# Moving the cast, the transposes and the load of the coming batches of x to a later place in one step of a fused attention and gated-FFN kernel

## Chip, cores and metric

The kernel runs on one core of one Trainium2 chip. The metric is the device time of one launch in microseconds (us), as the median of several runs. A profiled execution gives a trace beside it: what each engine did, and the core's span from the first to the last instruction.

## What is computed

For each of 8 batches x has 8 heads of 512 rows of 64 values, and a state has 8 heads of 32 rows. The attention goes both ways, and its joined result (544 rows a batch, 512 wide) goes through a gated FFN with 1536 hidden columns. Cut from the reference:

```python
scores = scale * np.matmul(x, state.transpose(0, 1, 3, 2))
a = softmax(scores)                      # x reads the state
xread = np.matmul(a, state)
scores2 = scale * np.matmul(state, x.transpose(0, 1, 3, 2))
a2 = softmax(scores2)                    # the state reads x
sread = np.matmul(a2, x)
x = concatenate([xread, sread], axis=2)  # then (batch, row, head * dim)
gate = 1.0 / (1.0 + np.exp(-(x @ w_gate)))
val = x @ w_val
out = (gate * val) @ w_out
```

`softmax` stands here for the maximum, exponential, sum and division of the original.

## The kernel before, in words

The rows that read the state are never multiplied with w_gate and w_val as rows of `xread`. The kernel forms `SW` (state times gate and value weights, `sw_wide`) for a batch, and multiplies it with the transposed attention `aT` (`gv_mm`, L283). So `gv_mm` of a batch needs that batch's `SW` and `aT`. Tanh on ScalarE (`gv_th`, L293) and a multiply on VectorE (`gv_glu`, L298) give `glu`, and `out_mm` (L314) multiplies it with w_out. The rows of all states' reads (`XS`) are a ninth batch at the end.

The order of the work is written out by hand. A first list (L425 to L690) handles batches 0 and 1 and the start of batch 2. Then a loop (L692) runs one step for each batch b from 2 to 8. A step has 12 groups, f = 0 to 11, one for each 128 hidden columns. A group issues `gv_mm(b, f)`, its tanh and multiply, and a third of a row block of `out_mm` of batch b - 1; where f is 0 or 6, half of `SW` of the next batch, nb = b + 1, comes first. Between them the step prepares the coming batches:

- `row(nb, t)`, six parts, t = 0 to 5: the scores (`S_mm`, L121, one half in t = 0 and the other in t = 1), maximum, subtraction and exponential, the sums and reciprocals (`n_sum`, L144 and L146), the multiply on GpSimd that gives `ab` (`n_mul`, L152), and last `aT_dma` (L173): four DMA transposes on SyncE's queue (SP), from `ab` to `aT`.
- `col(nb, t)`, five parts in f = 7 to 11: the scores the other way (`cT_mm`), exponential, a normalising multiply on GpSimd (`cT_nrm`, L204), and `c_dma` (L209): two DMA transposes on SP.
- `cast_x(nb + 1)`, two casts on GpSimd (L91) that wait for the load of that batch's x, and `at_xT_dma(nb + 1)`, four DMA transposes on SP (L113) that wait for the casts. Their result `xT` is what `S_mm` of that batch reads in the next step.
- `load_x(nb + 2)`, the load of a batch of x (1 MB, L74) on SP.
- `sr_mm(b)` and `sr_cp(b)`: the read of the state, 16 matmuls and two small copies.

In this trace GpSimd and SP's queue run their instructions in the order in which the list issues them, so one that waits holds up all that stand behind it. Outputs (`out_mm`, every third group) are also stored through SP (L320). In step 2 the code before has the groups of `row(3)` at f = 1 to 6, the casts and the transposes of batch 4 at f = 1, the load of batch 5 at f = 6. In step 3 it has `row(4)` at f = 0 to 5, the casts and the transposes of batch 5 at f = 1, and `sr_mm(3)` at f = 3 in the PSUM pool that the first scores use (`AT`). The load of batch 4 is issued just ahead of step 2 (L689).

Of the kernel before, what the change touches and what calls it, by code (L numbers as in the profile page):

```python
# [16 lines left out]
def kernel(  # L17
# [15 lines left out]
    B, H, S, D = x.shape  # L33
# [30 lines left out]
    AT, OU, GV, SWP = (p_at, "at"), (p_out, "outp"), (p_gv, "gv"), (p_sw, "swp")  # L64
# [5 lines left out]
    def load_x(b, eng, parts=1):  # L70
        xf = xfs[b] = stg.tile((128, H, 4, D), FP, name="xf")
        v, n = x[b].rearrange("h (p c) d -> p h c d", c=4), H // parts
        for i in range(parts):
            eng.dma_start(xf[:, n * i:n * i + n], v[:, n * i:n * i + n])  # L74
# [40 lines left out]
    def S_mm(b, i, place, jjs=(0, 1)):  # L115
        if jjs[0] == 0:
            held["S", b, i] = place[0].tile((128, 4, 2, 2, Ns), FP, name="Sp", tag=place[1])
        ps = held["S", b, i]
        for jj in jjs:
            for c in range(4):  # L120
                nc.tensor.matmul(ps[:, c, :, jj], xTs[b][:, 2 * i + jj, c], sTz[:, b, 2 * i + jj], start=True, stop=True)  # L121

    def S_max(b, i):

        if b not in E1s:
            E1s[b] = ap_.tile((128, 4, 2, 4, Ns), FP, name="E1")
        ps = held["S", b, i].rearrange("p c e j n -> p (c e) j n")
        mx = held["mx", b, i] = ap_.tile((128, 8, 2), FP, name="mx")
        nc.vector.tensor_reduce(mx, ps, AX.X, ALU.max)  # L129

    def S_sub(b, i):

        mx, ps = held["mx", b, i], held["S", b, i].rearrange("p c e j n -> p (c e) j n")
        nc.vector.tensor_tensor(halfE(b, i), ps, mx.unsqueeze(3).to_broadcast((128, 8, 2, Ns)), ALU.subtract)  # L134

    def S_exp(b, i):
        nc.scalar.activation(halfE(b, i), halfE(b, i), AF.Exp, scale=scale)  # L137
# [4 lines left out]
    def n_sum(b, i):  # L142
        rs = ap_.tile((128, 8, 2), FP, name="rs")
        nc.vector.tensor_reduce(rs, halfE(b, i), AX.X, ALU.add)  # L144
        ri = held["ri", b, i] = ap_.tile((128, 8, 2), FP, name="ri")
        nc.vector.reciprocal(ri, rs)  # L146

    def n_mul(b, i, eng, lo=0, n=4):
        if b not in abs_:
            abs_[b] = ap_.tile((128, 4, 2, 128), BF, name="ab")  # L150
        ri, ce = held["ri", b, i], slice(2 * lo, 2 * lo + 2 * n)
        eng.tensor_tensor(abs_[b].rearrange("p c e (j n) -> p (c e) j n", n=Ns)[:, ce, 2 * i:2 * i + 2],  # L152
                          halfE(b, i)[:, ce], ri[:, ce].unsqueeze(3).to_broadcast((128, 2 * n, 2, Ns)), ALU.mult)
# [17 lines left out]
    def aT_dma(b):  # L171
        for c in range(4):
            nc.sync.dma_start_transpose(aT_tile(b)[:, c], abs_[b][:, c].rearrange("p e k -> p (e k)"))  # L173
# [37 lines left out]
    def sr_mm(b, place):  # L211
        sr = held["sr", b] = place[0].tile((128, 4, 2, Ns), FP, name="srp", tag=place[1])
        Eb = Ebs[b].rearrange("p c e (j n) -> p c e j n", n=Ns)
        for j in range(4):
            for c in range(4):
                nc.tensor.matmul(sr[:, j], xbs[b][:, c, 2 * j:2 * j + 2].rearrange("p h d -> p (h d)"),  # L216
                                 Eb[:, c, :, j], start=(c == 0), stop=(c == 3))

    def sr_cp(b, e, cp):
        rows = slice(e * 64, (e + 1) * 64)  # L220
        cp(XS[rows, :, b * Ns:(b + 1) * Ns], held["sr", b][rows, :, e])
# [28 lines left out]
    def sw_wide(b, v):  # L250

        if b not in SWs:
            SWs[b] = fp.tile((128, 2, 2, dff), BF, name="SW", bufs=2)
        lo = 768 * v
        for k, places in enumerate(((OU, AT), (SWP, SWP), (SWP, SWP))):
            pss = [p[0].tile((128, 512), FP, name="swp", tag=p[1]) for p in places]
            if k < 2:
                sw_mm(pss, b, k, lo, 512, 0)
            else:
                for w in range(2):  # L260
                    sw_mm(pss, b, w, lo + 512, 256, 256 * w)
            for e in range(2):
                if k < 2:
                    sw_left[b, v, k, e] = (SWs[b][:, e, k, lo:lo + 512], pss[e])
                else:
                    sw_left[b, v, k, e] = (SWs[b][:, e, :, lo + 512:lo + 768], pss[e].rearrange("p (w n) -> p w n", w=2))

    def sw_cp(b, lo, w, e, cp):
        cp(*sw_left.pop((b, lo, w, e)))  # L269
# [5 lines left out]
    def gv_mm(b, f, place):  # L275
        n = n_of(b)
        fs = slice(f * 128, (f + 1) * 128)
        pss = []
        for w in range(2):
            ps = place[0].tile((128, 512), FP, name="gvp", tag=place[1])[:, :n]  # L280
            if b < B:
                for g in range(2):
                    nc.tensor.matmul(ps, SWs[b][:, g, w, fs], aTs[b][:, :, g], start=(g == 0), stop=(g == 1))  # L283
            else:
                for j in range(4):
                    nc.tensor.matmul(ps, (wg, wv)[w][:, j, fs], XS[:, j], start=(j == 0), stop=(j == 3))  # L286
            pss.append(ps)
        held["gv", b, f] = pss

    def gv_th(b, f):  # L290

        th = held["th", b, f] = fp.tile((128, 512), FP, name="th")[:, :n_of(b)]
        nc.scalar.activation(th, held["gv", b, f][0], AF.Tanh, scale=0.5)  # L293

    def gv_glu(b, f):
        if b not in glus:
            glus[b] = fp.tile((128, NF, n_of(b)), BF, name="glu", bufs=2, padded_shape=(128, NF, 512))
        nc.vector.scalar_tensor_tensor(glus[b][:, f], held["th", b, f], 1.0, held["gv", b, f][1], ALU.add, ALU.mult)  # L298
# [102 lines left out]
    def row(b, t):  # L401

        if t == 0:
            S_mm(b, 0, AT)
            S_max(b, 0)
        elif t == 1:
            S_sub(b, 0)
            S_mm(b, 1, SWP)
            S_max(b, 1)
        elif t == 2:  # L410
            S_sub(b, 1)
            S_exp(b, 0)
        elif t == 3:
            S_exp(b, 1)
            n_sum(b, 0)
            n_mul(b, 0, nc.gpsimd)
        elif t == 4:
            n_sum(b, 1)
            n_mul(b, 1, nc.gpsimd)
        else:  # L420
            aT_dma(b)
# [270 lines left out]
    for b in range(2, B + 1):  # L692
        nb = b + 1 if b + 1 < B else None
        for f in range(NF):

            v, q = divmod(f, 6)
            if nb is not None and q == 0:
                sw_wide(nb, v)
                sw_cp(nb, v, 0, 0, act)
                sw_cp(nb, v, 0, 1, act)  # L700
            ahead = nb is not None and q == 0
            for first in (ahead, not ahead):
                if first:
                    gv_mm(b, f, SWP if b == B and f % 2 else GV)
                    gv_th(b, f)
                    gv_glu(b, f)
                elif b < B or f < 9:
                    out_mm(b - 1, f)
            if nb is not None:
                if q == 0:  # L710
                    sw_cp(nb, v, 1, 0, vec)
                if q in (1, 3, 4):
                    k = max(q + 1, 3)
                    sw_cp(nb, v, k // 2, k % 2, act)
                if f == (4 if b > 2 else 10):
                    sr_cp(b, 0, act)
                    sr_cp(b, 1, vec)
                if 0 <= f - (b == 2) < 6:
                    row(nb, f - (b == 2))
                elif f >= 7:  # L720
                    col(nb, f - 7)
                if f == 6 and nb + 2 < B:
                    load_x(nb + 2, nc.sync, 4 if nb + 3 == B else 1)
                if f == 1 and nb + 1 < B:
                    cast_x(nb + 1, pool, 0, 4)
                    cast_x(nb + 1, pool, 4, 4)
                    at_xT_dma(nb + 1)
            if b < B and f == (3 if b > 2 else 9):
                sr_mm(b, AT if b > 2 else SWP)
            if b == B - 1:  # L730
                if f == 4:
                    sr_cp(b, 0, act)
                    sr_cp(b, 1, vec)
                for k in range(2):
                    if 0 <= f - 3 * k < 5:
                        col(k, f - 3 * k)
                    elif f == 8 + 3 * k:
                        sr_mm(k, SWP)
                        sr_cp(k, 0, act)
                        sr_cp(k, 1, vec)  # L740
# [33 lines left out]
```

## Time and profile before

| | us |
|---|---|
| median of 3 runs | 236.31 |
| lowest, highest | 235.29, 237.57 |
| the profiled execution, device time | 237.39 |
| its span, first to last instruction | 235.6 |
| TensorE busy in it | 224.3 |
| VectorE, ScalarE, GpSimd busy | 139.6, 144.0, 68.5 |

The device time of the profiled execution is 1.8 us more than its span, and 1.1 us more than the median of the runs. In the rows that follow, PE is TensorE, DVE is VectorE, ACT is ScalarE, POOL is GpSimd, and SPq is SyncE's DMA queue. A row of a timeline gives the start in us, the duration in us, the engine, the line of the kernel, the operation, output and input, the number of instructions, and in brackets the idle time before it with what ended it. The granted clock (PEclk) is the share of TensorE's full clock that it was given.

### The profile page before, as it was taken

Reading aid. Unit: us, or ns where it says so; the run is one execution under the profiler, and the core shown is the slowest. Engines: PE = TensorE matmul, PEld = TensorE weight load, DVE = VectorE, ACT = ScalarE, POOL = GpSimd, SP = SyncE. Lnnn points to the kernel's source line nnn. Section 1 sums busy time; section 2 is a strip of 40 time slices with the busy share of each in tenths; the row PEclk is TensorE's granted clock in tenths of the full one; section 3 lists DMA queues with packets and bytes.
Section 4 is the critical chain, followed back from the end, with each engine's and each line's share of the span. In section 5 each row is a group of like instructions: output and inputs, shape, how many; then the busy total and the mean of one; then the engine's idle time right before and its main releaser. Section 6 shows DMA issues by size and latency. Waiting matters only on the chain.

```text
span 235.6 us, 4975 instructions
## 1 busy us (share of the span) xinstructions
PE 224.3 (95%) x1887; PEld 112.4 (48%) x1887; DVE 139.6 (59%) x267; ACT 144.0 (61%) x290; POOL 68.5 (29%) x74
## 2 busy tenths in 40 slices
PE   5798999999999959999999999999999999999994
PEld 4674434444444424444444444444444444566754
DVE  3599889946586526754774567556765664432211
ACT  3679777957585825848485857585748555432311
POOL 4876180062024143303520261113110426100001
PEclk9999999999999979999999999999999999999999
DMA  6999969817553458527451665214122312311104
GB/s 205 273 200 289 180 99 188 236 36 200 127 177 67 136 138 220 156 49 268 83 143 37 178 167 123 69 56 92 46 70 67 90 57 79 89 45 67 69 22 114
DMA packets 47271, 29.49 MB, mean 125 GB/s; under 512 B 29872, under 2 KB 42544, under 8 KB 47248
## 3 DMA queue, kind: packets, MB, share of 16 engines
q1 hardware_dynamic: 40096, 21.84, 34.0%
q0 software_dynamic: 6864, 7.14, 16.4%
q10 hardware_dynamic: 288, 0.20, 0.5%
q8 instruction: 15, 0.25, 0.5%
q14 instruction: 8, 0.07, 0.1%
HBM read 18.35 MB, written 8.91 MB: 116 GB/s over the span
## 4 chain that ended last, share of the span: by engine, by line
PE 79%; DVE 6%; ACT 4%; DMA 3%; SPq 3%; issue 2%; POOL 2%; ACTq 0%; DVEq 0%; POOLq 0%
PE outp L314 33%; PE gvp L283 30%; PE gvp L286 5%; PE swp L231 4%; DVE glu L298 3%; DMA xf<-in_x_dram 2%; SPq L173 2%; ACT th L293 2%; PE Sp L121 2%; PE srp L216 1%; PE warm L348 1%; DVE rs L144 1%; PE outp L334 1%; PE cTp L181 1%; DMA aT<-ab 1%
## 5 line engine op out<-in xcount | busy, mean ns | idle before, releaser
L298 DVE SCALAR_TENSOR_TENSOR glu<-th,gvp 128x512 bf16<-128x512 f32 (+1 forms) x108 | 70.2, 657 | 72.2 <-ACT th L293 52.1
L283 PE MATMUL gvp<-aT,SW 128*128 128x512 bf16 x384 | 97.5, 379 | 3.3 <-DMA aT<-ab 2.5
L314 PE MATMUL outp<-wo,glu 128*128 128x512 bf16 x396 | 100.4, 384 | 0.0
L293 ACT ACTIVATE th<-gvp 128x512 f32<-128x512 f32 (+1 forms) x108 | 61.4, 575 | 56.2 <-PE gvp L283 46.7
L283 PEld LDWEIGHTS <-SW 128*128 128x128 bf16 x384 | 36.3, 98 | 49.3 <-issue 8.9
L314 PEld LDWEIGHTS <-glu 128*128 128x128 bf16 x396 | 37.1, 98 | 41.3 <-issue 3.4
L269 ACT CAST SW<-swp 128x512 bf16<-128x512 f32 x74 | 41.1, 587 | 4.0 <-PE swp L231 2.9
L204 POOL TENSOR_SCALAR cN<-cE,rc 128x512 bf16<-128x512 f32 x16 | 25.0, 1565 | 59.1 <-DVE rc L201 57.4
L318 ACT ACTIVATE res<-outp 128x512 f32<-128x512 f32 x33 | 19.7, 597 | 17.2 <-PE outp L314 17.0
L152 POOL TENSOR_TENSOR ab<-E,ri 128x512 bf16<-128x512 f32 x14 | 14.6, 1048 | 32.1 <-ACT E L137 15.3
L91 POOL CAST xb<-xf 128x1024 bf16<-128x1024 f32 (+1 forms) x13 | 12.5, 977 | 33.1 <-DMA xf<-in_x_dram 27.8
L269 DVE CAST SW<-swp 128x512 bf16<-128x512 f32 x22 | 14.7, 681 | 3.6 <-PE swp L231 3.6
L196 ACT ACTIVATE cE<-cTp,nb 128x512 f32<-128x512 f32 x16 | 11.1, 693 | 1.2 <-POOL cN L204 1.2
L129 DVE TENSOR_REDUCE mx<-Sp 128x16 f32<-128x512 f32 x16 | 10.9, 679 | 1.1 <-PE Sp L121 1.1
L134 DVE TENSOR_TENSOR E<-Sp,mx 128x512 f32<-128x512 f32 x16 | 11.0, 686 | 0.2
L188 DVE TENSOR_REDUCE cm<-cTp 128x1 f32<-128x512 f32 x16 | 10.9, 683 | 0.0
L144 DVE TENSOR_REDUCE rs<-E 128x16 f32<-128x512 f32 x16 | 10.8, 678 | 0.1
L137 ACT ACTIVATE E<-E 128x512 f32<-128x512 f32 x16 | 10.2, 639 | 0.5 <-DVE E L134 0.5
L325 POOL DMA_DIRECT2D out_dram<-res x2 | 1.1, 554 | 29.7 <-ACT res L318 29.7
L231 PE MATMUL swp<-wg,sTc 64*32 64x512 bf16 (+1 forms) x192 | 8.4, 328 | 0.1
L121 PEld LDWEIGHTS <-xT 128*128 128x128 bf16 x128 | 6.8, 108 | 3.2 <-issue 0.8
L231 PEld LDWEIGHTS <-sTc 64*32 64x32 bf16 x384 | 4.6, 91 | 7.4 <-issue 5.1
(62 smaller groups left out, 140.3 us busy)
## 6 DMA issues: line engine op xcount, KB each, us to landing
out_dram<-res SPq DMA_DIRECT2D x31, 256.0 KB, 2.4
xf<-in_x_dram SPq DMA_DIRECT2D x12, 256.0 KB, 4.6
xf<-in_x_dram SPq DMA_DIRECT2D x3, 1024.0 KB, 6.1
wo<-in_moe_w_out_dram POOLq DMA_DIRECT2D x3, 512.0 KB, 8.0
wv<-in_moe_w_val_dram POOLq DMA_DIRECT2D x2, 512.0 KB, 10.1
wg<-in_moe_w_gate_dram POOLq DMA_DIRECT2D x2, 512.0 KB, 9.8
xf<-in_x_dram POOLq DMA_DIRECT2D x2, 512.0 KB, 7.8
xf<-in_x_dram POOLq DMA_DIRECT2D x1, 1024.0 KB, 13.4
```

The costliest lines, as they stand in the source:

```text
L91: cp(xbs[b].rearrange("p c h d -> p h c d")[:, lo:lo + n], xfs[b][:, lo:lo + n])
L144: nc.vector.tensor_reduce(rs, halfE(b, i), AX.X, ALU.add)
L152: eng.tensor_tensor(abs_[b].rearrange("p c e (j n) -> p (c e) j n", n=Ns)[:, ce, 2 * i:2 * i + 2], halfE(b, i)[:, ce], ri[:, ce].unsqueeze ...
L204: eng.tensor_scalar(held["cN", b][:, e], held["cE", b, e], rc, None, op0=ALU.mult)
L231: nc.tensor.matmul(pss[e][j * Ns:(j + 1) * Ns, o:o + n], sTc[rows, b, j] if b > 1 else sTz[rows, b, j, e], (wg, wv)[w][rows, j, lo:lo + n] ...
L269: cp(*sw_left.pop((b, lo, w, e)))
L283: nc.tensor.matmul(ps, SWs[b][:, g, w, fs], aTs[b][:, :, g], start=(g == 0), stop=(g == 1))
L286: nc.tensor.matmul(ps, (wg, wv)[w][:, j, fs], XS[:, j], start=(j == 0), stop=(j == 3))
L293: nc.scalar.activation(th, held["gv", b, f][0], AF.Tanh, scale=0.5)
L298: nc.vector.scalar_tensor_tensor(glus[b][:, f], held["th", b, f], 1.0, held["gv", b, f][1], ALU.add, ALU.mult)
L314: nc.tensor.matmul(ops[b, c], glus[b][:, f, c * 128:(c + 1) * 128], wo[:, f], start=(f == 0), stop=(f == NF - 1))
L318: nc.scalar.activation(res, ops[b, c], AF.Copy, scale=0.5)
```

## The change

Only the loop changes. In step 2 the casts and transposes of x of batch 4 move from f = 1 to f = 6, where they stand behind `aT_dma(3)`, and the load of batch 5 moves from f = 6 to f = 8. In step 3 `row(4)` moves from f = 0 to 5 to f = 1 to 6, `sr_mm(3)` from f = 3 to f = 9 and from the pool `AT` to `SWP`, and `sr_cp(3)` from f = 4 to f = 10. All other steps stay. No instruction is added or taken away.

```diff
-                if f == (4 if b > 2 else 10):
+                if f == (4 if b > 3 else 10):
                     sr_cp(b, 0, act)
                     sr_cp(b, 1, vec)
-                if 0 <= f - (b == 2) < 6:
-                    row(nb, f - (b == 2))
+                if 0 <= f - (b < 4) < 6:
+                    row(nb, f - (b < 4))
                 elif f >= 7:
                     col(nb, f - 7)
-                if f == 6 and nb + 2 < B:
+                if f == (6 if b > 2 else 8) and nb + 2 < B:
                     load_x(nb + 2, nc.sync, 4 if nb + 3 == B else 1)
-                if f == 1 and nb + 1 < B:
+                if f == (1 if b > 2 else 6) and nb + 1 < B:
                     cast_x(nb + 1, pool, 0, 4)
                     cast_x(nb + 1, pool, 4, 4)
                     at_xT_dma(nb + 1)
-            if b < B and f == (3 if b > 2 else 9):
-                sr_mm(b, AT if b > 2 else SWP)
+            if b < B and f == (3 if b > 3 else 9):
+                sr_mm(b, AT if b > 3 else SWP)
```

In the issue order of the engines this gives, for steps 2 and 3: on POOL the two multiplies (L152) of batch 3 now stand ahead of the two casts of batch 4. On SP the order before was load 4, four transposes xT(4), two stores, four transposes aT(3), load 5, two stores, two transposes of batch 3's other scores, four transposes xT(5). It becomes load 4, two stores, four transposes aT(3), four transposes xT(4), a store, load 5, a store, two transposes of batch 3's other scores, four transposes xT(5).

## Prediction

> **What bounds the kernel now.** I read the page first, then TensorE's waits, then the chain of waits around the one long wait, then the clock in that place.
>
> ```profile
> span 235.6 us, 4975 instructions
> PE 224.3 (95%) x1887; PEld 112.4 (48%) x1887; DVE 139.6 (59%) x267; ACT 144.0 (61%) x290; POOL 68.5 (29%) x74
> PEclk9999999999999979999999999999999999999999
> PE 79%; DVE 6%; ACT 4%; DMA 3%; SPq 3%; issue 2%; POOL 2%; ACTq 0%; DVEq 0%; POOLq 0%
> ```
>
> TensorE is the bound: 95% busy, 79% of the chain that ended last. One slice of the clock's 40 stands at 7, the fifteenth, from 82.5 to 88.4 us. TensorE's own waits name the cause:
>
> ```profile
> PE gvp L283 <- DMA aT<-ab: 2.5, 1, 2.5
> ```
>
> That is the longest wait of TensorE in the run, and it happens once, at the start of step 3. The chain shows it:
>
> ```profile
> 82.58 2.38 DMA aT<-ab
> ...
> 85.09 1.02 PE gvp L283 x4
> 86.11 1.70 PE outp L314 x4
> ...
> 88.24 1.50 PE outp L314 x4
> 89.74 0.86 PE gvp L283 x4
> ```
>
> The last transpose of aT(3) is issued at 82.58 and lands 2.38 us later; `gv_mm(3, 0)` starts at 85.09. Then four output matmuls take 1.70 and 1.50 us, where four take 0.86 elsewhere. So the wait is paid twice: idle, and then at a low clock. The windows give the clock:
>
> ```profile
> 85.00:88.00 3.00, 2.91 (x16) 1.37 (x17) 1.29 (x2) 0.60 (x1) 0.00 (x0) 0.67 0.69 205
> 88.00:91.00 3.00, 3.00 (x23) 1.45 (x21) 0.85 (x2) 0.79 (x2) 0.82 (x1) 0.77 1.03 333
> ```
>
> After the stretch the columns are its length, the five engines' busy time, the clock (0.67, 0.77), the DMA share and GB/s. The loss is 3.0 x 0.33 + 3.0 x 0.23 = 1.68 us.
>
> Why aT(3) is late stands in SP's queue:
>
> ```profile
> 63.20 0.57 SPq L74 DMA_DIRECT2D xf<-in_x_dram  x1
> 71.45 5.13 SPq L113 DMA_TRANSPOSE xT<-xb  x4
> 76.68 1.00 SPq L320 DMA_DIRECT2D out_dram<-res  x2
> 77.78 6.04 SPq L173 DMA_TRANSPOSE aT<-ab  x4
> 83.93 0.52 SPq L74 DMA_DIRECT2D xf<-in_x_dram  x1
> ...
> 92.23 5.12 SPq L113 DMA_TRANSPOSE xT<-xb  x4
> 97.45 1.00 SPq L320 DMA_DIRECT2D out_dram<-res  x2
> 100.09 5.05 SPq L173 DMA_TRANSPOSE aT<-ab  x4
> ```
>
> Load 4 (63.20) is awaited by the casts; SP stands at the transposes of xT(4) until 71.45, spends 5.13 us issuing them and 1.00 on two stores, and only at 77.78 starts aT(3). GpSimd has the same knot:
>
> ```profile
> 69.40 2.02 POOL L91 CAST xb<-xf 128x1024 bf16<-128x1024 f32 x2 [14.38 <-DMA xf<-in_x_dram]
> 71.39 2.06 POOL L152 TENSOR_TENSOR ab<-E,ri 128x512 bf16<-128x512 f32 x2
> 90.18 2.02 POOL L91 CAST xb<-xf 128x1024 bf16<-128x1024 f32 x2 [5.33 <-PE gvp L283]
> 99.01 1.05 POOL L152 TENSOR_TENSOR ab<-E,ri 128x512 bf16<-128x512 f32 x1 [1.59 <-DVE ri L146]
> ```
>
> **The change part by part.** First, aT(3) goes ahead of xT(4). VectorE gives the last reciprocal that `ab` needs here:
>
> ```profile
> 71.36 0.25 DVE L146 RECIPROCAL ri<-rs 128x16 f32<-128x16 f32 x1
> ```
>
> It ends at 71.61, and 0.15 us later (as 98.61 + 0.25 to 99.01 has it in the next step) the second multiply can start; the first, free of the casts, is done by then. At 1.05 us each `ab` is ready at 72.8, against 73.45 before. The two stores of the step's early groups are gone by then: the second's result is written here,
>
> ```profile
> 68.92 0.60 ACT L318 ACTIVATE res<-outp 128x512 f32<-128x512 f32 x1
> ```
>
> and a store's issue takes 0.5. SP starts aT(3) at 72.9. Its fourth issue begins 3.9 us later, at 76.8, and lands 2.4 later, at 79.2. The four swp groups end at 85.09 - 2.52 = 82.57, so the slack is 3.4 us where 2.52 was missing. The whole wait goes, and with it the low clock that followed.
>
> Second, xT(4) goes behind it. The casts on GpSimd start at 72.8 (load 4 had landed by 69.40) and end at 74.8, hidden behind SP's issue of aT(3), which ends at 78.0. The transposes run from 78.1 to 83.2; the fourth is issued at about 82.0 and lands at 84.5. Who needs it is `S_mm(4, 0)`, now in group 1 of step 3. What TensorE does in the steps:
>
> ```profile
> 58.49 1.04 PE L283 MATMUL gvp<-aT,SW 128*128 128x512 bf16 x4
> ...
> 61.95 0.40 PE L121 MATMUL Sp<-sTz,xT 128*128 128x64 bf16 x8
> ...
> 81.72 0.41 PE L231 MATMUL swp<-wg,sTc 64*32 64x512 bf16 x8
> ...
> 85.09 1.02 PE L283 MATMUL gvp<-aT,SW 128*128 128x512 bf16 x4 [2.52 <-DMA aT<-ab]
> ```
> ```profile
> 110.10 0.41 PE L231 MATMUL swp<-wg,sTc 64*32 64x512 bf16 x8
> ...
> 110.88 1.04 PE L283 MATMUL gvp<-aT,SW 128*128 128x512 bf16 x4
> ...
> 134.24 0.41 PE L231 MATMUL swp<-wg,sTc 64*32 64x512 bf16 x8
> ```
>
> In step 2 the scores in group 1 come 61.95 - 58.49 = 3.46 us after the step's first matmul. In step 3 they are then due at 82.57 + 3.46 = 86.0: slack 1.5 us. Cost nothing, but this is what is late next.
>
> Third, load 5 moves behind xT(4) and a store: 83.2 + 0.6 = 83.8, where it started at 83.93. So its landing, the casts at 90.18, xT(5) at 92.23 and the two stores to 98.45 stay. `ab` of batch 4 was ready at 100.06 (99.01 + 1.05); with the row of step 2's pattern it comes 72.8 - 58.49 = 14.3 us after the step's start, at 96.9. So SP sets aT(4): issued from 98.5, its fourth at 102.3, landed at 104.7. It is due at 82.57 + 23.23 + 0.78 = 106.6 (the step's length is next; 0.78 is 110.88 - 110.10). Slack 1.9 us, where it was 4.6. Cost nothing.
>
> Fourth, the row and `sr` of step 3 take step 2's places. From first gv to the next step's swp: step 2 took 81.72 - 58.49 = 23.23, step 3 took 110.10 - 85.09 = 25.01, step 4 took 134.24 - 110.88 = 23.36. Step 3 is 1.65 longer than step 4, the low clock by another road (1.68 above). The new pattern is worth 23.36 - 23.23 = 0.13 more. It could cost instead: step 2's neighbours differ, so I bound it by -0.13 and +0.13 and take the gain, since the issue order of step 3 becomes that of step 2.
>
> The sum: 2.52 idle + 1.65 clock + 0.13 = 4.30 us. The span becomes 231.3, the profiled execution 237.39 - 4.30 = 233.1. That execution lay 1.08 above the median of the runs, so for the median 236.31 - 4.30 = 232.0 us.
>
> The Trainium skill, page "TensorE: Matmul & The Clock Gate", section "Why this matters for your kernels", speaks against the second term: to keep the clock, no idle gaps over about 3 us between bursts, since one idle window halves it. This trace differs: a gap of 2.52 us was followed by clocks of 0.67 and 0.77. By that rule the clock would not be at stake and the gain would be 2.65.
>
> **The rivals.**
> A, the forecast: 232.0.
>
> B, the low clock is not there in most runs. It shows in one execution, which lay above the median, and the three runs spread over 2.3 us. Then only 2.52 + 0.13 goes: 236.31 - 2.65 = 233.7. Against it: the trace has the low clock right behind the gap, and the clock is full in the steps beside it. The same page ("What's actually happening") says that the window runs free of the kernel, so whether a gap is caught varies; no run here shows that yet.
>
> C, SP is late and another wait takes the place of the one removed. Four transposes do not always take 5.05:
>
> ```profile
> 172.50 6.21 SPq L173 DMA_TRANSPOSE aT<-ab  x4
> ```
> ```profile
> DMA to landing us min/median/max: 2.4/2.5/4.2
> ```
>
> The first row is of SP's queue for aT(7), the second of the xT transposes, from issue to landing. Were aT(3) and xT(4) both 1.16 longer, xT(4) would land at 86.8, 0.8 late; with the longest landing, 1.7 more, 2.5 late. `gv_mm(4, 0)` with its 1.9 slack has four such groups ahead: if three are long, 3.5 - 1.9 = 1.6 late. So 0.8 to 2.5 us comes back: 232.8 to 234.5, about 233.5 in the middle. Against it: both have over 1 us in hand at the usual durations.
>
> D, slower. Load 5 lands late and, as GpSimd and SP both wait for it in order, `ab` and aT(4) come late with it.
>
> ```profile
> xf<-in_x_dram SPq DMA_DIRECT2D x3, 1024.0 KB, 6.1
> ...
> xf<-in_x_dram POOLq DMA_DIRECT2D x1, 1024.0 KB, 13.4
> ```
>
> If it took 13.4 us, 7.3 more, TensorE would wait 7.3 - 1.9 = 5.4 at step 4 and lose the clock's 1.65 again: 7.0 - 4.3 = 2.7 slower, 239.0. It decides from 4.3 - 1.65 + 1.9 = 4.6 us of delay. Against it: SP's own loads take 6.1, the slow one was another queue's, and load 5 is issued at the same moment as before with the same neighbours.
>
> E, no change: aT(3) is late for another reason than its place in the queue. Against it: SP's order, GpSimd's order and the reciprocal's end leave none. 236.3.
>
> **How the numbers follow.** A 0.66, B 0.14, C 0.12, D 0.05, E 0.03. The forecast is A: 232.0. The range reaches down 1.0 for the spread of medians (the runs shown differ by 2.3) and up to 234.4, which takes in B and nearly all of C; D, E and the edges, under 2 in 10, are left out. A measurement of this kernel can tell about 1% from no change, 2.4 us. Faster by more (below 233.9): A, two thirds of B and half of C, 0.82. Within 1%: the rest of B and C and E, 0.13. Slower: D, 0.05.
>
> **What would show it.** Step 1 is right if the wait of `gvp` for aT is gone and the first gv of step 3 starts right behind the swp, near 82.6; the clock of the following windows is then 1.00. Step 2 is right if the scores in group 1 of step 3 start without a wait of TensorE for xT. Step 3 is right if load 5 is issued near 83.8 and the first gv of step 4 waits for nothing, near 106.6. Step 4 is right if step 3 takes 23.2 from gv to swp. A wait of TensorE in group 1 of step 3 or at the start of step 4 would be C or D; a slow clock elsewhere, or a median near 233.7 with the gap gone, would be B.

## The result and the profile after

The changed kernel takes 234.65 us (median of 11 runs, 233.37 to 235.43), the kernel before 236.69 in the same comparison: a ratio of 0.9911, with a 95% interval of 0.9883 to 0.9939. That is 2.1 us faster, where 4.3 were forecast; 234.65 lies above the range. Some executions of both kernels run in a slower state (in one trace of the kernel before the clock is 0.95 nearly from end to end); the ratios, their intervals and the counts of runs below leave them out, the medians in us do not.

The profiled execution after took 233.37 us, which makes it the fastest of the 11 runs. Three lines of its page:

```profile
span 231.5 us, 4975 instructions
PE 221.2 (96%) x1887; PEld 110.0 (48%) x1887; DVE 139.2 (60%) x267; ACT 144.0 (62%) x290; POOL 68.6 (30%) x74
PEclk9999999999999999999999999999999999999999
```

The 7 in the clock's row is gone. SP's queue after (start, duration, line, operation):

```profile
72.31 5.04 SPq L173 DMA_TRANSPOSE aT<-ab  x4
77.45 5.75 SPq L113 DMA_TRANSPOSE xT<-xb  x4
...
83.94 0.39 SPq L74 DMA_DIRECT2D xf<-in_x_dram  x1
...
92.52 5.45 SPq L113 DMA_TRANSPOSE xT<-xb  x4
...
99.17 5.07 SPq L173 DMA_TRANSPOSE aT<-ab  x4
104.35 0.52 SPq L74 DMA_DIRECT2D xf<-in_x_dram  x1
...
106.81 3.23 SPq L209 DMA_TRANSPOSE Eb<-cN  x2
```

The order is the one of the change: aT(3) at 72.31, then xT(4), then load 5 at 83.94. TensorE's timeline after, at the places that the prediction named:

```profile
57.19 0.41 PE L231 MATMUL swp<-wg,sTc 64*32 64x512 bf16 x8
57.97 1.04 PE L283 MATMUL gvp<-aT,SW 128*128 128x512 bf16 x4
...
81.98 1.04 PE L283 MATMUL gvp<-aT,SW 128*128 128x512 bf16 x4
...
85.44 0.40 PE L121 MATMUL Sp<-sTz,xT 128*128 128x64 bf16 x8
...
105.21 0.41 PE L231 MATMUL swp<-wg,sTc 64*32 64x512 bf16 x8
...
105.99 1.04 PE L283 MATMUL gvp<-aT,SW 128*128 128x512 bf16 x4
...
114.18 0.63 PE L216 MATMUL srp<-Eb,xb 128*128 128x64 bf16 x16 [0.65 <-DMA Eb<-cN]
```

From the first gv of step 2 to that of step 4 it takes 105.99 - 57.97 = 48.02 us; before it took 110.88 - 58.49 = 52.39. So the four steps of the prediction brought 4.37 us in this execution, against 4.30 worked out. The last row is new: in group 3 of step 4 the read of the state by batch 4 (`sr_mm(4)`) waits for the two transposes of its `Eb`. The read is also shown before the change, with SP's queue and the time from issue to landing of its two transposes:

```profile
105.25 0.52 SPq L74 DMA_DIRECT2D xf<-in_x_dram  x1
...
111.25 3.30 SPq L209 DMA_TRANSPOSE Eb<-cN  x2
```
```profile
DMA to landing us min/median/max: 2.7/3.4/4.0
```
```profile
118.26 0.63 PE L216 MATMUL srp<-Eb,xb 128*128 128x64 bf16 x16
```

Before, the second of the two is issued at 112.99 and lands 2.7 us later, at 115.7, so the read has 2.6 us in hand. The rest of the question is what the new wait costs, and what other executions look like.

### The profile page after: what moved, and what is told of

Read it like the earlier page. It is cut to its first block, busy times and chain, and to the rows that moved or that the text cites. A ratio compares the mean times of both kernels' runs of the same rounds, so it can differ in the third digit from the quotient of the medians.

```text
span 231.5 us, 4975 instructions
## 1 busy us (share of the span) xinstructions
PE 221.2 (96%) x1887; PEld 110.0 (48%) x1887; DVE 139.2 (60%) x267; ACT 144.0 (62%) x290; POOL 68.6 (30%) x74
## 4 chain that ended last, share of the span: by engine, by line
PE 74%; DMA 9%; ACT 6%; DVE 3%; POOL 3%; issue 2%; SPq 1%; ACTq 0%; POOLq 0%; DVEq 0%
PE outp L314 33%; PE gvp L283 27%; PE gvp L286 5%; DMA wo<-in_moe_w_out_dram 4%; PE swp L231 4%; DMA xf<-in_x_dram 2%; DMA Eb<-cN 2%; DVE glu L298 2%; PE srp L216 2%; ACT th L293 1%; POOL cN L204 1%; ACT SW L269 1%; ACT E L137 1%; PE cTp L181 1%; PE outp L334 1%
## 5 line engine op out<-in xcount | busy, mean ns | idle before, releaser
L314 PE MATMUL outp<-wo,glu 128*128 128x512 bf16 x396 | 98.9, 379 | 0.4 <-DMA wo<-in_moe_w_out_dram 0.4
L152 POOL TENSOR_TENSOR ab<-E,ri 128x512 bf16<-128x512 f32 x14 | 14.6, 1048 | 40.3 <-DVE ri L146 29.8
L121 PEld LDWEIGHTS <-xT 128*128 128x128 bf16 x128 | 6.3, 103 | 3.2 <-ACT xT L108 0.4
```

Source lines behind the costliest of these rows:

```text
L314: nc.tensor.matmul(ops[b, c], glus[b][:, f, c * 128:(c + 1) * 128], wo[:, f], start=(f == 0), stop=(f == NF - 1))
```

## The experiments

Each ratio compares a kernel with the kernel before on the same chip; the chips differ from one group of experiments to the next.

**The kernel before once more, and a filled gap.** The first was unchanged.

> The kernel before, unchanged, for a second trace and the granted clock of each run. Two theories for why the median fell by about 2.1 us (0.9911 of 236.69) where steps 2 to 4 of the two traces differ by 4.37 - 0.80 = 3.57 us. Theory W (a new wait): every execution of the kernel before has the wait of about 2.5 us and the low clock; then the mean clock of nearly all runs is near 0.993, as in the first trace (1.68 us of 235.6 is 0.7%), and the second trace has a wait of 2.2 us or more. Theory V (the removed cost varies): in most executions TensorE reaches step 3 later against SP's queue, the wait is shorter and often leaves the clock alone; then most runs have a mean clock of 0.997 or more, and the second trace has a wait under 2 us or no window below 0.95 behind it.

Measured: 0.9985 (0.9949 to 1.0022). Of the 22 runs of the kernel before on the other side of this comparison, 15 had a mean clock of 0.991 to 0.993 and 7 one of 0.999 or 1.000. Of the 9 on this side, the same kernel, 3 had a low one; on two other chips it was 13 of 17 and 10 of 16. So about two executions in three (41 of 64) pay the low clock, neither all nor few. A second trace:

> The kernel before once more, one look. Its wait for aT of batch 3 at the start of step 3: 2.0 to 3.5 us, and a granted clock under 0.9 in one of the two windows of 3 us behind it, as about three quarters of its runs have a mean clock near 0.992. A trace with a mean clock of 1.000 would show what the wait is where the clock is kept.

Measured: 236.38 us, mean clock 0.992, and this wait, and these windows (length, five engines' busy time, clock, DMA share, GB/s):

```profile
PE gvp L283 <- DMA aT<-ab: 2.4, 1, 2.4
```
```profile
84.00:87.00 3.00, 2.71 (x7) 1.02 (x8) 0.74 (x2) 0.60 (x1) 0.17 (x1) 0.50 0.70 204
87.00:90.00 3.00, 3.00 (x29) 1.55 (x27) 1.35 (x3) 0.74 (x2) 0.60 (x1) 0.93 0.94 308
```

The clock loses 3.0 x 0.50 + 3.0 x 0.07 = 1.7 us, as in the first trace. The filled gap:

```diff
+            if b == 3 and f == 0:
+                warm(20, GV)
             ahead = nb is not None and q == 0
```

> The kernel before with 20 matmuls of 128 columns on constants (about 0.1 us each, 2.0 us) put into the place where TensorE waits for aT of batch 3; their result is read by nothing. The wait for aT stays, TensorE is busy in it, so the clock should not fall. It measures the clock term alone. If the low clock comes in every execution (theory W): 1.65 us faster, 0.993. If it comes in few (theory V): within 0.5 us of the kernel before, 0.998 to 1.003, or slower where the wait is shorter than 2.0 us.

Measured: 235.11 us, 0.9940 (0.9912 to 0.9968), 1.4 us faster. The 20 matmuls take 1.3 us instead of the 2.0 estimated. The trace keeps a clock of 1.00 in the window behind the gap although TensorE still waits there:

```profile
PE gvp L283 <- DMA aT<-ab: 1.3, 1, 1.3
```
```profile
85.00:88.00 3.00, 3.00 (x29) 1.64 (x28) 2.06 (x5) 1.07 (x2) 0.00 (x0) 1.00 0.93 317
```

So work that computes nothing, put into an idle stretch, makes this kernel faster. The clock term was real: 1.4 us of the median, where one execution showed 1.65. Part of what the clock was worth is already given back here: in this trace the read of batch 3 waits 0.57 us for its `Eb`, a wait that neither of the two traces of the kernel before shown here has.

**The changed kernel in more executions.**

> The changed kernel, unchanged, for a second trace. Its first trace is of its fastest run (233.37, median 234.65) and has a wait of 0.65 us of TensorE in step 4, where the 16 matmuls of the state's read of batch 4 wait for transposes that were issued behind load 6. Theory W: in a run near the median that wait is longer, 1.5 to 2.5 us. Theory V: it stays at 0.3 to 1.2 us, and the runs differ ahead of step 2, in the first list: the start of step 2, 57.97 in the first trace, moves by 1 us or more. Against the kernel before: 0.985 to 0.995 by both.

Measured: 0.9924 (0.9889 to 0.9959); the traced execution took 234.96 us. Its timeline of TensorE and SP's queue:

```profile
56.89 0.41 PE L231 MATMUL swp<-wg,sTc 64*32 64x512 bf16 x8
...
107.92 1.02 PE L283 MATMUL gvp<-aT,SW 128*128 128x512 bf16 x4 [2.16 <-DMA aT<-ab]
...
115.75 0.63 PE L216 MATMUL srp<-Eb,xb 128*128 128x64 bf16 x16 [0.30 <-DMA Eb<-cN]
```
```profile
77.15 6.33 SPq L113 DMA_TRANSPOSE xT<-xb  x4
...
92.76 6.15 SPq L113 DMA_TRANSPOSE xT<-xb  x4
...
100.12 5.34 SPq L173 DMA_TRANSPOSE aT<-ab  x4
```

Neither theory had this: a second new wait, 2.16 us for aT of batch 4, stands at the start of step 4. It is the removed wait, one step later. The read's own wait is short here because TensorE comes to it late already. Two more traces tested what sets the time then.

> The changed kernel once more, one look. If the read of the state in step 4 sets the time, the run is as long as that read's first matmul is late: the two traces so far have it at 114.18 with 233.37 us and at 115.75 with 234.96, that is 119.2 us more in both, whether the wait for aT of batch 4 is 0 or 2.16. Expected: start of the read plus 119.2, within 0.4. If other waits set it, the two numbers do not go together.

> The same, a fourth trace of the changed kernel: start of the read in step 4 plus 119.2 us, within 0.4.

Measured: reads at 114.57 and 115.21 (waits of 1.44 and 1.48 us for `Eb`), so 233.8 and 234.4 expected; 233.96 and 234.32 came out. In all four traces the read's start and the run's time go together, whatever the waits ahead of it. The two traces of the kernel before, whose read waits for nothing, give the same sum (118.26 + 119.1 and 117.32 + 119.1). So this places the differences between executions ahead of the read; it does not yet show that the read's wait makes them. In the last two traces the first gv of step 4 waits too, 0.22 and 0.84 us. The profile names a cast of `SW` on ScalarE as what ended these waits, but in the first trace of the changed kernel that gv starts (105.99) in the middle of the same casts (105.68 to 106.75). The last transpose of aT(4) lands 0.1 us ahead of the gv in both (103.11 and 103.71, each 2.4 us to landing), so they are read here as waits for aT(4). Theory V's start of step 2 moved by 0.7 us at most (swp at 56.49 to 57.19).

**The read later, and the load behind.** Two kernels take the read of step 4 out of the way from two sides. The first moves the read:

```diff
-                if f == (4 if b > 3 else 10):
+                if f == (4 if b > 4 else 10):
...
-            if b < B and f == (3 if b > 3 else 9):
-                sr_mm(b, AT if b > 3 else SWP)
+            if b < B and f == (3 if b > 4 else 9):
+                sr_mm(b, AT if b > 4 else SWP)
```

> The changed kernel with the state's read of batch 4 moved as well, from group 3 to group 9 of step 4 (in the PSUM pool that steps 2 and 3 use), some 11 us later, so that its transposes have landed behind load 6 long before. Theory W: the wait was what was given back, so the median falls by 0.8 us at the least and up to 2 below the changed kernel's, to about 0.980 of the kernel before. Theory V: it falls by the 0.65 to 0.9 us of the trace at most, to about 0.988.

Measured: 232.90 us (232.70 to 233.22), 0.9833 (0.9798 to 0.9868). The changed kernel in the same comparison had 0.9924, so moving the read gains 0.9%, about 2.2 us: as much as had been given back. The runs now lie within 0.5 us of each other. The traces show less of it: from the first swp of step 2 to the end of the span this one takes 174.1 us, the four of the changed kernel 175.6 in the mean. Its own first gv of step 4 still waits 0.81 us, read as above as a wait for aT(4). The second moves load 6:

```diff
-                if f == (6 if b > 2 else 8) and nb + 2 < B:
+                if f == (6 if b > 3 else 11 if b == 3 else 8) and nb + 2 < B:
```

> The changed kernel with one thing moved: load 6 is issued in group 11 of step 3, behind the two transposes of batch 4 that the state's read waits for, instead of ahead of them. The read stays in group 3 of step 4. Theory (those transposes land 5 to 7 us after their issue because the load stands ahead of them in the same queue): they land 2.4 to 3 us after it, near 111.5, and the read, due near 113.5, waits for nothing. The casts of batch 6 on GpSimd wait for the later load and hold up the multiplies of batch 5 behind them, so aT of batch 5 may come 0 to 2 us late for step 5. Rival (the transposes are slow by themselves, or by the stores): they still take over 5 us, and the wait for them stays.

Measured: 234.32 us, 0.9937 (0.9905 to 0.9970). The time from issue to landing of the two transposes, first in the changed kernel, then here:

```profile
DMA to landing us min/median/max: 5.2/6.0/6.8
```
```profile
DMA to landing us min/median/max: 3.3/3.7/4.0
```

and TensorE's timeline here:

```profile
57.55 0.41 PE L231 MATMUL swp<-wg,sTc 64*32 64x512 bf16 x8
...
113.73 0.63 PE L216 MATMUL srp<-Eb,xb 128*128 128x64 bf16 x16
...
132.30 1.02 PE L283 MATMUL gvp<-aT,SW 128*128 128x512 bf16 x4 [1.75 <-DMA aT<-ab]
```

Without the load ahead of them the transposes land in 3.3 to 4.0 us and the read waits for nothing; the rival is out. They do not land in the 2.4 to 3 us that the theory had. The price is the one foreseen: aT of batch 5 is now 1.75 us late, and the gain is about spent. This trace also gives the read's due time: with no wait of TensorE ahead of it, it starts 113.73 - 57.55 = 56.18 us after the first swp of step 2.

**One part alone.** Only the queue's order changes; the scores of batch 4 and the read of batch 3 stay where they were.

```diff
-                if f == 6 and nb + 2 < B:
+                if f == (6 if b > 2 else 8) and nb + 2 < B:
...
-                if f == 1 and nb + 1 < B:
+                if f == (1 if b > 2 else 6) and nb + 1 < B:
```

> One part of the change alone: in step 2 the casts and transposes of batch 4 and load 5 move behind aT of batch 3, while the scores of batch 4 stay in group 0 and the state's read of batch 3 stays in group 3 of step 3. Theory (the wait moves along one chain: SP's queue has not become faster, TensorE only reaches the next user of it sooner): the wait at the start of step 3 goes, but the scores in group 0 wait for xT of batch 4 by about 0.5 to 2 us (landing near 84.5 to 86, due near 83.8), and the read in group 3 (due near 89.5) waits for two transposes issued behind load 5 that land near 92: in all 2 to 3 us come back, 0.992 to 0.997 of the kernel before. Rival (only the place of aT mattered, nothing else is late): 0.982, as the prediction's sum has it.

Measured: 235.65 us, 0.9948 (0.9934 to 0.9963), with both waits that the theory named:

```profile
85.14 0.32 PE L121 MATMUL Sp<-sTz,xT 128*128 128x64 bf16 x5 [0.96 <-DMA xT<-xb]
92.77 0.63 PE L216 MATMUL srp<-Eb,xb 128*128 128x64 bf16 x16 [1.90 <-DMA Eb<-cN]
```

So the shift of the scores and of the read in step 3 is no decoration: it is what keeps step 3 free of waits, and the read of step 4, which was not shifted, meets the same wait for `Eb`.

**What lengthens a group of transposes.** Three fillers of the first list are issued as twice as many matmuls of half the columns, on top of the late read:

```diff
-    warm(16, GV)
+    warm(32, GV, 64)
...
-    warm(12, SWP)
+    warm(24, SWP, 64)
...
-    warm(15, GV)
+    warm(30, GV, 64)
```

> The kernel with the state's read of batch 4 in group 9, whose trace still has a wait of 0.81 us for aT of batch 4 at the start of step 4, with three of the idle-time fillers of the first list issued as twice as many matmuls of half the columns: 43 pairs of weight load and matmul more on TensorE, for about the same time. In all five traces the DMA transposes whose issue takes 1.4 us or more rather than 1.2 stand beside a 16 KB packet of the instruction queue, about 15 in a run, so one for each 128 pairs; in the step at issue two of them hit xT(4) and xT(5). 43 pairs earlier is about 5 us earlier: one hits aT(3), the next falls where SP issues no transposes. Theory (the fetch is what lengthens a group of transposes): one group fewer is long, aT of batch 4 lands about 1.1 us sooner, the wait of 0.81 goes, 0.3 to 0.8 us faster than 232.9. Rival (the long groups come from the load of x or the stores beside them): the same groups are long, the wait stays, 232.9.

Measured: 235.94 us, 0.9948 (0.9915 to 0.9981). As a time this missed: step 2 starts 2.9 us later in this trace (59.93 against 57.08). The finer fillers themselves put TensorE 0.9 us behind (the last of them starts at 17.36 against 16.46). Most of the rest is a new wait in the first list:

```profile
39.09 0.32 PE L121 MATMUL Sp<-sTz,xT 128*128 128x64 bf16 x5 [2.41 <-DMA xT<-xb]
```
```profile
36.00:39.00 3.00, 0.68 (x6) 0.32 (x4) 1.58 (x3) 0.64 (x2) 0.00 (x0) 1.00 1.30 170
39.00:42.00 3.00, 2.86 (x24) 1.31 (x33) 2.01 (x4) 1.71 (x3) 0.00 (x0) 1.00 1.24 208
```

The last transpose of that xT is issued at 31.6 (30.2 with the late read alone) and lands after 7.4 us instead of at most 4.2, while loads of GpSimd's queue are in flight; why it is so late was not tested. The clock stays at 1.00 in this gap and behind it. In 4 of the 9 counted runs of this kernel the mean clock is 0.992, in none of the 5 with the late read alone. The mechanism that the experiment asked about is seen in SP's queue, first with the late read alone, then with the fetches moved:

```profile
72.20 5.04 SPq L173 DMA_TRANSPOSE aT<-ab  x4
77.34 6.43 SPq L113 DMA_TRANSPOSE xT<-xb  x4
...
92.91 6.28 SPq L113 DMA_TRANSPOSE xT<-xb  x4
```
```profile
75.05 6.48 SPq L173 DMA_TRANSPOSE aT<-ab  x4
81.63 5.14 SPq L113 DMA_TRANSPOSE xT<-xb  x4
...
96.10 5.12 SPq L113 DMA_TRANSPOSE xT<-xb  x4
```

The long groups moved with TensorE's instruction count, to aT(3); the neighbours on the queue are the same in both. The first of the two kernels has the wait of 0.81 us at the start of step 4, the second has none; as its step 2 also starts later, this last difference does not prove the theory.

**The order carried further.** In the diff of the change the bounds on b go up by one, or to the last step:

> The change carried one step further: step 3 too issues aT of batch 4 ahead of the casts and transposes of batch 5, and load 6 in group 8; step 4 too has the scores one group later and the state's read in group 9. Theory (each step that keeps the old order after the change meets the late queue): the waits for aT of batch 4 and for the transposes behind load 6 go, and the first step in the old order, 4, has more in hand than step 3 had or meets the same wait one step later, 0 to 2 us: 0.980 to 0.986. Rival (the queue is full, so the wait only grows on the way): 0.990 or more.

> The order that the change gives step 2 used in all steps, 2 to 6: aT first, then the casts and transposes of the batch after, then the load in group 8, the scores one group later and the state's read in group 9. Theory: no step has the old order, so no user is reached early; no wait of TensorE behind step 2 is left, 0.978 to 0.983, with runs close together as in the kernel with the late read (0.5 us). Rival: the order itself costs in each step (the transposes of the scores the other way stand behind the load): a wait in each of steps 4 to 7, 0.990 or more.

Measured: 233.00 us, 0.9866 (0.9836 to 0.9896), and 232.80 us (232.11 to 233.44), 0.9836 (0.9817 to 0.9855). Both lie just above what the theories had, and the runs of the second spread over 1.3 us instead of 0.5. With one step more, the read of step 5 waits 0.16 us and the scores of step 4 wait 0.46; in the other kernel this is the longest wait of TensorE behind step 2:

```profile
109.20 0.32 PE L121 MATMUL Sp<-sTz,xT 128*128 128x64 bf16 x5 [0.39 <-DMA xT<-xb]
```

Both this and the late read alone (0.9833) lie below the interval of the changed kernel; their own intervals do not tell them apart.

## Why the prediction was wrong: it followed the queue to the start of step 4 and no further

First step, aT(3) ahead of xT(4): right. It starts at 72.31, 14.34 us after the first gv of step 2; worked out was 72.9, or 14.4 after it. The wait and the low clock are gone.

Second step, xT(4) behind it: right. The scores start 85.44 - 81.98 = 3.46 us after the first gv of step 3 and wait for nothing.

Fourth step, the length of step 3: right. From first gv to the next swp it takes 105.21 - 81.98 = 23.23 us, as worked out.

Third step, "load 5 moves behind xT(4) ... cost nothing": this failed, in two ways. The smaller: aT(4) was to start at 98.5 and have 1.9 us in hand. It started at 99.17 to 100.12, because the groups xT(4) and xT(5) took 5.45 to 6.33 us instead of 5.13. In one trace its last transpose also took 3.6 us to land instead of 2.4, and the gv came 2.16 us late. This is what rival C described, with its slack and its long groups; with 0.12 it was given too little, as a long group was taken for chance. In all four traces both groups are long, and one 16 KB packet of an instruction queue stands beside each. The prediction's own rows had such a group: aT(3) took 6.04, with a packet at 80.13. The packet now comes at 78.6 to 79.8, when xT(4) is being issued. The next came at 99.38 before, beside the stores; now it comes at 93.4 to 94.5, in xT(5).

The larger: the step stopped at aT(4). It found that SP's chain up to there keeps its absolute times while TensorE comes 4.3 us sooner, and did not follow that to load 6 (105.25 before, 104.35 after) and to the user behind it. Before, the read of step 4 had 2.6 us in hand, less than the gain. Now it comes due 4.9 us sooner (56.18 us after the first swp of step 2, so at 113.4 in the first trace after). The second of its transposes is issued 4.2 us sooner, at 108.80, as `cN` is ready sooner too; but the two now stand 1.9 to 2.5 us behind load 6 instead of 6.0, and the second lands after 5.2 to 6.3 us instead of 2.7. No rival named the read.

The size: measured from the first swp of step 2, the read starts at 56.99, 58.86, 58.05 and 58.72 us in the four traces of the changed kernel, so 0.81, 2.68, 1.87 and 2.54 us late, 1.98 in the mean. The waits for `Eb` are 0.97 us of that mean, those at the start of step 4 0.81. The sum of 4.30 less 1.98 is 2.3; the ratio says 2.1. In the two traces of the kernel before it starts at 60.54 and 60.29, so 4.4 and 4.1 us late by the same yardstick, which is the forecast gain. The first trace after is of the fastest run of 11, so it shows less of this than the median pays.

Rival B, no low clock in most runs, does not explain it: the filled gap is 1.4 us faster, and the clock is low in about two runs in three. On the rule of the Trainium skill, page "TensorE: Matmul & The Clock Gate", section "Why this matters for your kernels" (no idle gaps over about 3 us), the measurement decides: gaps of 2.52 and 2.40 us were followed by windows of 0.67 and 0.50. In other kernels gaps of 2.16 and 1.75 us left the windows behind them at 1.00, and so did the 2.41 us in the kernel with the finer fillers. So the length of the gap alone does not decide, and rival B was right that the clock is not lost each time. In about one run in three of the kernel before it is kept; what decides it was not tested. By the rule of about 3 us alone the gain would have been 2.65; that this lies near the 2.1 measured is chance.

Rivals D and E did not come: load 5 landed in 6.2 to 6.4 us, and aT(3) was late for its place in the queue alone.

What stays open: whether the wait for aT(4) occurs in most executions (0, 2.16, 0.22 and 0.84 us in the four traces), why the late read gains 2.2 us of the median where the traces differ by 1.5, and why it also narrows the spread of the runs to 0.5 us in five runs.

## What to carry to other kernels

When a wait is removed, the engine that waited arrives sooner at everything behind it, while the queue that made it wait keeps its times wherever TensorE does not set them: follow the queue to each of its later users, and check the slack of each, until it is larger than the gain. A large load issued shortly ahead of small transfers on one queue delayed their landing here, so a user that had 2.6 us in hand had none. Take slacks from several executions, and expect a trace of the best run to hide what the median pays.

## What the runs showed of the hardware that was not expected

DMA transposes of aT and xT on SP usually take 1.2 to 1.3 us each to issue; now and then one takes 1.6 to 2.7. In the 14 traces there are 70 such long ones, and each overlaps a packet of 16 KB on an instruction queue. Of the 577 that overlap none the longest took 1.53; 25 overlap one and stay under 1.5. The transposes of `Eb` reach 2.0 us behind a load without such a packet, so not every long transpose has one, as the expectation above had it. In the kernel before, from the chain of waits and from the DMA view of the window from 80 to 81 us (queue, packets, MB, share of the 16 engines):

```profile
80.31 2.22 SPq L173
```
```profile
q8 instruction: 1, 0.02, 8.5%
```

There are 15 such packets in a run of 3774 instructions of TensorE, so one for each 250, and shifting that count by 86 instructions shifted the long groups, as shown above. That the packet is TensorE's instruction fetch is inferred from these counts; that it holds up a transpose in flight is what the moved fetch speaks for.

The pair of `Eb` transposes behind a 1 MB load on the same queue takes 4.7 to 7.8 us from issue to landing when the first is issued 1.2 to 2.5 us after the load, and 2.7 to 4.0 when it is 6 us after it. With the load issued behind the pair it is 3.3 to 4.0.
